# One attention and two expert layers on one core: q and k copied out in key order, the log rows loaded already repeated, and every task of the attention with its own rank and engine

## The chip, the core and the metric

The kernel runs on one core of a Trainium2 chip. The metric is the device time of one execution in microseconds (us); for the kernel before there are three timed runs, and one more execution was profiled.

The engines are named as in the profile: PE is TensorE (its matrix products; its weight loads are listed as PEld), DVE is VectorE, ACT is ScalarE, POOL is GpSimd, and SP is SyncE, which issues nearly all transfers. Each engine runs its own list of instructions in a fixed order; if the instruction at the head of a list waits, everything behind it waits too.

## The reference

Attention over 2 batches of 8 heads, 576 positions and 64 columns, with a bias made by a small network from the distance of two positions; the result goes as 1152 rows of 512 through two layers of two matrix products each (512 to 2048 and back). Cut to what matters:

```python
def _attn_ref(q, k, v, w1, b1, w2):
    scores = scale * np.matmul(q, k.transpose(0, 1, 3, 2))
    psi_rel = np.log1p(np.abs(rel))
    psi_i = np.log1p(np.maximum(pos[:, None], 1.0))
    x = (psi_rel / psi_i)[..., None]
    h = np.maximum(x @ w1 + b1, 0.0)
    bias = h @ w2
    scores = scores + bias.transpose(2, 0, 1)[None, :, :, :]
    attn = softmax(scores)
    return np.matmul(attn, v)

def _moe_ref(x, w_in, w_out, s, b):
    r = np.maximum(x @ w_in, 0.0)
    return (s * (r * r) + b) @ w_out

def _moe2_ref(x, w_in, w_out):
    h = x @ w_in
    sp = log1p(exp(min(h, 20)))
    return (h * np.tanh(sp)) @ w_out
```

Everything is 32-bit floating point at the interface. Each weight of the two layers arrives in 64 bits and is turned into two 32-bit parts on the core.

## The kernel before

**The bias.** The bias depends on the positions only. It is made in 36 groups of 16 query positions (G). For a group, four "rows" are made (`bias_row`, lines 261 to 271: a ReLU of the log row `lx` plus a column of `bl`, 128 partitions by 304 to 576 columns), then PE multiplies them by `w2b` (`bias_products`, L281, in one or two pieces), then the product is copied out of PSUM with a factor (`bias_out`, the tile `bo`; its instruction stands at the helper's lines L172 or L174/L176), then the part on the other side of the diagonal is a mirrored copy inside `bo` (`bias_mirror`, also L172), and then `bo` is stored to memory (`bias_store`, L307, tensor `nbias_d`). It is read back in another layout as `nb` (`load_bias`, L323) when a unit of the attention needs it.

**The start.** Two log rows of 576 numbers are loaded into one partition each (L225). PE spreads them over 128 partitions by a product with ones (L242), and the small network's weights likewise (`c`, L236); DVE and ACT copy these out and scale them (L243 to L251, L172, L176).

**The pairs.** Two heads of one batch make a pair; there are eight. q and k of a pair are loaded (`raw`, L354; for the first two pairs straight into `nat`, L350), regrouped by one copy on ACT (`pack`, `nat` from `raw`), turned by PE (`turn`, L389, tile `t`), and copied out to `qk` (`put`, lines 394 to 402). Column t·64+p of the turned tile belongs to key p·9+t, so the copy reorders: before, it reads PSUM straight through and writes to SBUF with a step of nine elements.

**The units.** A unit is a pair and a tile of queries: tiles 0 to 3 have 128 queries, tile 4 has 64, of which both heads are taken together. There are 40 units. For each: scores on PE (L428, tile `s`), bias and minimum on DVE (L438, tile `mn`), exponential and its sum on ACT (L448, tile `e`), the sum's reciprocal on POOL and DVE (L455, L459, tile `rs`), division on POOL (L465), turning on PE (L480, tile `pp`, and L481/L483, tile `pr`), the copies out (`keep`, tile `pt`; `keep_rest`, tile `prt`; on DVE or ACT), the product with V on PE (L508, tile `po`), and the split of the result into a high and a low part (`xh` on ACT, L528; `xl` on DVE, L168). V is loaded by four transfers a pair (`natv`, L374 and L376: two of 128 KB and two of 16 KB for the last 64 keys), with two clearings on POOL (L371, L372).

**The layers.** Two layers of 48 blocks: products into `h` (L830), an activation on ACT and DVE, products into `y` (L907). Four blocks' first products stand among the last units of the attention.

**What sets the order.** All of it is a list of tasks with an engine, an estimated duration, a rank, the tasks it comes after and the buffers it takes. A planner (`Plan.run`, lines 590 to 623) walks through them: of all tasks that could start, the one that can start first is next, and among equals the one with the lowest rank. The instructions are written out in that order, and each engine keeps it. Before, a task's rank is ten times its unit's number plus a constant of its kind (`RANK`), and the engine of a copy comes from a short repeated pattern:

```python
    ROWS = ('vvav',)
    KEEPS = 'avv'
    OUTS = 'aaa'
    PUTS = 'avv'
```

Here `a` stands for ACT, `v` for DVE, `p` for POOL. So every `bias_out` is on ACT, and of 36 mirrored copies all but the last.

## Time and profile before

| | before |
|---|---|
| median of three runs | 607.04 us (603.47 to 608.15) |
| the profiled execution, its own time | 607.61 us |
| its span in the profile | 605.8 us |
| PE busy | 582.0 us (96%), 4732 matrix instructions |
| DVE busy | 477.0 us (79%) |
| ACT busy | 379.8 us (63%) |
| POOL busy | 86.6 us (14%) |
| moved by DMA | 65.41 MB, mean 108 GB/s |

The span runs from the first to the last instruction of the profile; the execution's own time is 1.8 us more. PE's busy time covers matrix products that overlap in its pipeline, so a stretch in which PE is busy all the time may still hold fewer products than it could. The chain of waits that ends last runs through PE's products of the two layers.

### The profile page before, as it was taken

How to read it: one execution, taken by the hardware profiler on the slowest of the kernel's cores; microseconds unless marked ns; L12 is line 12 of the kernel's file. 1: busy time of each engine (PE TensorE's matmuls, PEld its weight loads, DVE VectorE, ACT ScalarE, POOL GpSimd, SP SyncE). 2: the span in 40 equal slices, each digit the busy share in tenths (PEclk: the TensorE clock that was granted, in tenths of full speed). 3: DMA queues.
4: the chain of work that ended last, by engine and by line, in shares of the span. 5: the costliest groups of instructions: out<-in, count | busy, mean ns of one | idle time of the engine just before them, and what ended most of it. 6: DMA issues, size and time to landing. Idle time of an engine off the chain costs nothing. (4 is left out here: it accounts for less than half of the span.)

```text
span 605.8 us, 12603 instructions
## 1 busy us (share of the span) xinstructions
PE 582.0 (96%) x4732; PEld 511.0 (84%) x4732; DVE 477.0 (79%) x1052; ACT 379.8 (63%) x802; POOL 86.6 (14%) x209
## 2 busy tenths in 40 slices
...
GB/s 98 229 232 256 153 199 153 194 224 169 133 93 102 243 252 252 270 61 1 0 2 1 83 232 240 244 36 1 2 1 0 53 1 1 2 52 1 1 1 52
DMA packets 50064, 65.41 MB, mean 108 GB/s; under 512 B 17490, under 2 KB 34002, under 8 KB 50004
## 3 DMA queue, kind: packets, MB, share of 16 engines
...
q14 instruction: 23, 0.19, 0.1%
q10 hardware_dynamic: 192, 0.09, 0.1%
...
## 5 line engine op out<-in xcount | busy, mean ns | idle before, releaser
L465 POOL TENSOR_SCALAR e<-e,rs 128x576 f32<-128x576 f32 (+2 forms) x104 | 69.0, 680 | 33.9 <-DVE rs L459 29.8
L830 PE MATMUL h<-xh,whi 128*128 128x384 f32 x192 | 64.8, 338 | 0.0
L830 PE MATMUL h<-yh,wli 128*128 128x384 f32 x192 | 64.7, 337 | 0.0
L830 PE MATMUL h<-yl,whi 128*128 128x384 f32 x192 | 64.6, 337 | 0.0
L830 PE MATMUL h<-yh,whi 128*128 128x384 f32 x192 | 64.6, 336 | 0.0
L830 PE MATMUL h<-xh,wli 128*128 128x384 f32 x192 | 64.4, 336 | 0.0
L830 PE MATMUL h<-xl,whi 128*128 128x384 f32 x192 | 64.4, 336 | 0.0
L438 DVE CUSTOM_DVE_ANT_0 s<-s,nb 128x576 f32<-128x576 f32 x72 | 51.9, 753 | 9.2 <-PE s L428 8.1
L428 PE MATMUL s<-qk 64*128 64x144 f32 (+1 forms) x640 | 51.3, 301 | 7.1 <-ACT qk L172 5.4
L428 PEld LDWEIGHTS s<-qk 64*128 64x128 f32 (+1 forms) x640 | 42.0, 179 | 18.8 <-issue 6.8
L448 ACT ACTIVATE e<-s,mn 128x576 f32<-128x576 f32 x72 | 55.5, 772 | 3.1 <-DVE mn L438 2.5
L859 ACT ACTIVATE r<-n,two 128x384 f32<-128x384 f32 x48 | 29.5, 616 | 43.7 <-DVE n L855 43.7
L843 DVE SCALAR_TENSOR_TENSOR u<-h,u 128x384 f32<-128x384 f32 x48 | 26.6, 555 | 36.9 <-ACT u L840 36.8
L271 DVE TENSOR_SCALAR r<-lx,bl 128x528 f32<-128x528 f32 (+17 forms) x108 | 47.4, 486 | 5.5 <-PE bias L281 5.4
L840 ACT ACTIVATE u<-h 128x384 f32<-128x384 f32 x48 | 23.3, 485 | 43.3 <-PE h L830 43.3
L281 PE MATMUL bias<-r,w2b 128*32 128x264 f32 (+17 forms) x352 | 41.0, 526 | 4.8 <-DVE r L271 2.0
L907 PE MATMUL y<-gl,who 128*128 128x384 f32 (+1 forms) x192 | 44.6, 338 | 0.0
L851 ACT ACTIVATE u<-u 128x384 f32<-128x384 f32 x48 | 25.1, 523 | 31.0 <-DVE u L848 30.9
L907 PE MATMUL y<-gh,wlo 128*128 128x384 f32 (+1 forms) x192 | 44.3, 337 | 0.0
L907 PE MATMUL y<-gh,who 128*128 128x384 f32 (+1 forms) x192 | 44.3, 337 | 0.0
L907 PE MATMUL y<-who,gh 128*128 128x512 f32 x144 | 43.3, 395 | 0.9 <-ACT y L919 0.9
L907 PE MATMUL y<-wlo,gh 128*128 128x512 f32 x144 | 43.3, 395 | 0.0
...
## 6 DMA issues: line engine op xcount, KB each, us to landing
...
nb<-nbias_d SPq DMA_DIRECT2D x32, 288.0 KB, 3.3
...
raw<-in_q_dram SPq DMA_DIRECT2D x6, 288.0 KB, 4.0
raw<-in_k_dram SPq DMA_DIRECT2D x6, 288.0 KB, 4.8
```

Source lines behind the costliest of these rows:

```text
L271: engine.tensor_scalar(r, src, bl[:, g : g + 1], 0.0, op0=ALU.add, op1=ALU.max)
L281: nc.tensor.matmul(ps[32 * a : 32 * a + 32], w2b.rearrange("p h i -> p (h i)"), rows[G, a][:, c0:c1], start=True, stop=True)
L428: nc.tensor.matmul(self.ps[rows, x if self.both else 2 * j + x, o : o + PIECE], st.qk[d, 0, self.q0 : self.q0 + self.w], st.qk[d, 1, c0 : ...
L438: nc.vector.tensor_tensor_reduce(out=self.s[n][:m], in0=self.ps[:m, 2 * n : 2 * n + 2, :HALF], in1=nb[:m].rearrange("p (n j) -> p n j", n= ...
L448: nc.scalar.activation(out=self.e[:m, (S + REST) * n :][:, :S], in_=self.s[n][:m].rearrange("p n j -> p (n j)"), func=AF.Exp, bias=self.mn ...
L465: nc.gpsimd.tensor_scalar(self.e[:m, y : y + w], self.e[:m, x : x + w], self.rs[:m, n : n + 1], 0.0, op0=ALU.mult, op1=ALU.add)
L830: nc.tensor.matmul(self.ph, w[:, c * P : (c + 1) * P], x[:, c, :], start=(c == 0 and n == 0), stop=(c == KD - 1 and n == 2),)
L840: nc.scalar.activation(out=self.u, in_=self.ph, func=AF.Relu)
L843: nc.vector.scalar_tensor_tensor(self.u, self.ph, 0.0, self.u, op0=ALU.max, op1=ALU.mult)
L851: nc.scalar.activation(out=self.z, in_=self.z, func=AF.Exp)
L859: nc.scalar.activation(out=self.r, in_=self.n, func=AF.Ln, bias=two)
L907: nc.tensor.matmul(o, a, c, start=(f == 0 and i == 0), stop=(f == NF - 1 and i == 2))
```

## The change

- The log rows and the small weights are loaded by transfers that read the same source again for each partition (`spread`), so that the start needs no product on PE; scaling is on DVE, and `w2b` is filled by four small copies on POOL.
- `put` reads PSUM with a step of 64 elements and writes `qk` straight through, where it read straight through and wrote with a step of nine.
- The last 64 keys of V of both heads of a pair come in one transfer of 128 partitions (`lastv`), and POOL copies them to their places and clears the rest (`spread_v`); before, two transfers went straight there.
- The last part of a unit's turning is a task of its own (`turn_rest`).
- Each task of the attention has its own addition to its rank (`SHIFT`, one character a task, six units a step) and each copy its own engine (`WHO`). The order of the units, several leads and ranks, and the planner's durations are other numbers.

What is computed is the same. In the tables of the diff only a line or two stand.

```diff
-    ROWS = ('vvav',)
-    ROWS0 = ('vvva',)
-    KEEPS = 'avv'
-    RESTS = 'va'
-    OUTS = 'aaa'
-    PUTS = 'avv'
-    PACKS = 'a'
+    WHO = {
...
+        'bias_out': 'vvaaaaavvvvaaaaaaaaaavavaaaaaavaavavaavvvavv',
...
+        'put': 'avaaavavavavavvvvaaa',
...
+    SHIFT = {
...
+        'bias_out': '+/++@-+,7(<+?`7>Vb/J1]8Su5`:,EUu118UC2SL/g9^',
...
+    SSTEP = 6
-    ORDER = ((4, 2), (4, 0), (4, 3), (0, 3), (0, 0), (4, 1), (3, 1), (0, 2), (1, 1), (0, 1), (1, 2), (3, 2), (3, 3), (2, 2), (2, 3), (2, 1), (2, 0), (1, 3), (1, 0), (3, 0))
+    ORDER = ((4, 2), (4, 0), (4, 1), (0, 2), (0, 1), (4, 3), (3, 1), (3, 3), (1, 1), (0, 0), (1, 2), (0, 3), (1, 0), (2, 1), (2, 0), (1, 3), (2, 2), (2, 3), (3, 2), (3, 0))
...
-    NLEAD = 7
+    NLEAD = 5
...
-    FREE = {"PE": 5.6, "ACT": 5.9, "DVE": 5.4, "POOL": 1.5, "SP": 2.1, "none": 0.0}
+    FREE = {"PE": 4.0, "ACT": 5.0, "DVE": 5.4, "POOL": 4.5, "SP": 2.4, "none": 0.0}
...
-    R0 = 9
-    MIRR0 = 35
...
-    WSTEP = 0.89
+    WSTEP = 1.19
...
-    WEARLY = ('i0', 'o0', 'i2', 'o1', 'i1', 'o3', 'o2', 'i3')
+    WEARLY = ('i2', 'o0', 'i1', 'i0', 'o3', 'o1', 'i3', 'o2')
...
-    FRANK = 8
+    FRANK = 2
...
-    GRANK = -443
+    GRANK = -487
...
-    VRANK = 507
+    VRANK = 413
...
-    c1 = bp.tile([HID, 2 + H], F32, name="c1")
     c3 = bp.tile([P, 2 + H], F32, name="c3")
     w1c, b1c = c3[:, 0:1], c3[:, 1:2]
-    lx1 = [rp.tile([1, S], F32, tag="r", name=f"lx1_{n}") for n in range(2)]
-    for n in (1, 0):
-        nc.sync.dma_start(out=lx1[n], in_=ins["c_lx"][n : n + 1])
+
+    def spread(engine, out, src, ap):
+        engine.dma_start(out=out, in_=bass.AP(tensor=src.tensor, offset=src.offset, ap=ap))
+
     with nc.allow_non_contiguous_dma(reason="a few short columns"):
-        nc.sync.dma_start(out=c1[:, 0:1], in_=ins["w1"].rearrange("o (c e) -> (o c) e", e=1))
-        nc.sync.dma_start(out=c1[:, 1:2], in_=ins["b1"].rearrange("(c e) -> c e", e=1))
-        nc.scalar.dma_start(out=c1[:, 2:], in_=ins["w2"])
-    nc.scalar.dma_start(out=liall, in_=ins["c_li"])
+        spread(nc.scalar, w1c, ins["w1"], [[0, RI], [1, HID], [1, 1]])
+        spread(nc.sync, lx[1], ins["c_lx"][1:2], [[0, P], [1, S]])
+        spread(nc.scalar, b1c, ins["b1"], [[0, RI], [1, HID], [1, 1]])
+        nc.scalar.dma_start(out=liall, in_=ins["c_li"])
+        spread(nc.sync, c3[:, 2:], ins["w2"], [[0, RI], [H, HID], [1, H]])
+        spread(nc.sync, lx[0], ins["c_lx"][0:1], [[0, P], [1, S]])
     nc.scalar.preload_act_table_set("natural_log_exp_and_others")
     w2b = bp.tile([P, H, RI], F32, name="w2b")
-    nc.gpsimd.memset(w2b, 0.0)
-    c4 = ps1("c4")[:, : 2 + H]
-    for i in range(RI):
-        nc.tensor.matmul(c4[HID * i : HID * i + HID], ident[:HID, :HID], c1, start=True, stop=True)
-    lx2 = ps4("lx2")
-    ones = rp.tile([1, P], F32, tag="bo", name="ones", bufs=BUFS["bo"])
-    nc.gpsimd.memset(ones, 1.0)
-    for n in (1, 0):
-        for x in range(2):
-            nc.tensor.matmul(lx2[:, 2 * n + x, :HALF], ones, lx1[n][:, x * HALF : x * HALF + HALF], start=True, stop=True)
-    nc.vector.tensor_copy(c3, c4)
-    for i in range(RI):
-        rows = slice(i * HID, (i + 1) * HID)
-        copy("a", w2b[rows, :, i], c4[rows, 2:])
     bl = bp.tile([P, NG], F32, name="bl")
-    nc.vector.tensor_scalar_mul(bl, li, b1c)
-    for n, who in ((1, "v"), (0, "a")):
-        copy(who, lx[n].rearrange("p (x s) -> p x s", x=2), lx2[:, 2 * n : 2 * n + 2, :HALF], w1c)
+    with tc.manual_schedule(engines={mybir.EngineType.DVE, mybir.EngineType.Pool}):
+        nc.gpsimd.memset(w2b, 0.0)
+        nc.vector.tensor_scalar_mul(lx[1], lx[1], w1c)
+        nc.vector.tensor_scalar_mul(bl, li, b1c)
+        nc.vector.tensor_scalar_mul(lx[0], lx[0], w1c)
+        for i in range(RI):
+            rows = slice(i * HID, (i + 1) * HID)
+            nc.gpsimd.tensor_scalar(w2b[rows, :, i], c3[rows, 2:], 1.0, 0.0, op0=ALU.mult, op1=ALU.add)
...
-    def bias_row(G, a):
+    def bias_row(G, a, who):
...
-        who = row_engine(G, a)
...
-    def bias_out(G, c0, c1):
+    def bias_out(G, c0, c1, who):
...
-        copy(OUTS[G % len(OUTS)], bo[G][:, b0 + c0 : b0 + c1], bo[G, c0], ninv[:, G : G + 1])
...
+        copy(who, bo[G][:, b0 + c0 : b0 + c1], bo[G, c0], ninv[:, G : G + 1])
-    def bias_mirror(G):
+    def bias_mirror(G, who):
...
-        if gorder.index(G) < MIRR0:
+        if who == "a":
...
-            nc.gpsimd.memset(a[REST:, FULL, 0, :], 0.0)
-            nc.gpsimd.memset(a[: P - REST, FULL, 1, :], 0.0)
             for j in range(2):
                 nc.sync.dma_start(out=a[:, :FULL, j, :], in_=s2[j, : FULL * P, :].rearrange("(t p) d -> p t d", p=P))
+            self.last_v = natp.tile([P, D], F32, tag="lastv", name=f"lastv_{self.name}")
+            nc.sync.dma_start(out=self.last_v, in_=s2[:, FULL * P :, :])
+            self.v = a
+
+        def spread_v(self):
             for j in range(2):
-                nc.sync.dma_start(out=a[REST * j : REST * j + REST, FULL, j, :], in_=s2[j, FULL * P :, :])
-            self.v = a
+                for x in range(2):
+                    rows = slice(ROW * x, ROW * x + ROW)
+                    if x == j:
+                        nc.gpsimd.tensor_scalar(self.v[rows, FULL, j, :], self.last_v[rows], 1.0, 0.0, op0=ALU.mult, op1=ALU.add)
+                    else:
+                        nc.gpsimd.memset(self.v[rows, FULL, j, :], 0.0)
...
-            to = self.qk.rearrange("d x (p t) -> d x t p", t=DEAL)
+            to = self.qk.rearrange("d x (p t) -> d x p t", t=DEAL)
             if x == 2:
-                copy(who, to[:, :, DEAL - 1], self.last.rearrange("d (x p) -> d x p", x=2))
+                copy(who, to[:, :, :, DEAL - 1], self.last.rearrange("d (x p) -> d x p", x=2))
             elif self.wide:
                 ps = self.ps.rearrange("d n c -> d (n c)")[:, 2 * BANK * x :][:, :S]
-                copy(who, to[:, x], ps.rearrange("d (t p) -> d t p", p=SD))
+                copy(who, to[:, x], ps.rearrange("d (t p) -> d p t", p=SD))
             else:
-                copy(who, to[:, x, : DEAL - 1], self.ps[:, x].rearrange("d (t p) -> d t p", p=SD))
+                copy(who, to[:, x, :, : DEAL - 1], self.ps[:, x].rearrange("d (t p) -> d p t", p=SD))
...
-            self.pr = ps1(f"pr_{self.name}")
...
+        def turn_rest(self):
+            self.pr = ps1(f"pr_{self.name}")
...
         def add(self, engine, us, rank, f, *args, after=(), takes=(), mb=0.0):
+            what = f.__qualname__.split("<locals>.")[-1]
+            n = self.count[what] = self.count.get(what, -1) + 1
+            if what in SHIFT and n < len(SHIFT[what]):
+                rank += SSTEP * (ord(SHIFT[what][n]) - ord("P"))
             t = Task(engine, us, rank, f, args, after, takes, self.LAGS[engine], mb)
+            t.what, t.ways = what, None
             self.tasks.append(t)
+            return t
+
+        def add_any(self, ways, rank, f, *args, **more):
+
+            what = f.__qualname__.split(".")[-1]
+            n = self.count.get(f.__qualname__.split("<locals>.")[-1], -1) + 1
+            who = WHO[what][n % len(WHO[what])]
+            t = self.add(*ways[who], rank, f, *args, who, **more)
+            t.ways = ways
             return t
...
-            add(*(("ACT", 0.0008 * w + 0.1) if row_engine(G, a) == "a" else ("DVE", 0.0007 * w + 0.05)), at - 15 + a,
-                bias_row, G, a, after=[], takes=[hs[a]])
+            add_any({"a": ("ACT", 0.00083 * w + 0.19), "v": ("DVE", 0.0007 * w + 0.05)}, at - 15 + a, bias_row, G, a, takes=[hs[a]])
...
-        m = add(*(("ACT", 0.0008 * (BW - w) + 0.15) if x < MIRR0 else ("POOL", 0.0008 * (BW - w) + 0.25)), at + GRANK + 2, bias_mirror, G, after=outs)
-        stores[G] = add("SP", 0.38, at - 50, bias_store, G, after=[m], mb=0.3)
+        m = add_any({"a": ("ACT", 0.0008 * (BW - w) + 0.1), "p": ("POOL", 0.0012 * (BW - w) + 0.15)}, at + GRANK + 2, bias_mirror, G, after=outs)
...
-                valued[u.hp, u.b] = add("SP", 1.85, 10 * i + VRANK, stacks[u.hp, u.b].load_v, after=[load], mb=0.4)
-                valued[u.hp, u.b].past = [s]
+                hl = Hold("lastv")
+                lv = add("SP", 1.9, 10 * i + VRANK, stacks[u.hp, u.b].load_v, after=[load], takes=[hl], mb=0.4)
+                lv.past = [s]
+                valued[u.hp, u.b] = add("POOL", 0.5, 10 * i, stacks[u.hp, u.b].spread_v, after=[lv])
+                hl.users.append(valued[u.hp, u.b])
...
-        t = add("PE", 0.68 if u.n == 2 else 0.54, at + RANK["turn"], u.turn, after=ds, takes=[hp, hr])
+        t = add("PE", 0.49 if u.n == 2 else 0.27, at + RANK["turn"], u.turn, after=ds, takes=[hp])
+        t1 = add("PE", 0.13 if u.n == 2 else 0.24, at + RANK["turn"] + 1, u.turn_rest, after=ds, takes=[hr])
```

What this does to the order of the instructions, at three places. Line numbers differ between the two kernels (L281 is L308 after, L389 is L423, L428 is L462, L480/L481 are L513/L517, L508 is L544, L268 is L295, and the helper's L172 is L207). Of names like `s_0_2_2962` the first two numbers are the pair's heads and the query tile, the last is a running number; both batches have the same name.

The first instructions of PE, before:

```order
L1081 UNCONDITIONAL_BRANCH
L242 MATMUL lx_134<-lx_1_119,ones 128x288 x2
L242 MATMUL lx_134<-lx_0_118,ones 128x288 x2
L236 MATMUL c_129<-c_116,ident 32x10 x4
L281 MATMUL bias_0_179<-r_169,w2b 32x264
L281 MATMUL bias_0_179<-r_171,w2b 32x264
```

and now:

```order
L1129 UNCONDITIONAL_BRANCH
L308 MATMUL bias_0_166<-r_151,w2b 32x264
L308 MATMUL bias_0_166<-r_156,w2b 32x264
L308 MATMUL bias_0_166<-r_158,w2b 32x264
L308 MATMUL bias_0_166<-r_162,w2b 32x264
```

The eight products that spread the rows and the weights are gone; the first bias group is PE's first work.

The first instructions of ACT after its table load, before (`bo` from `bias` is a copy out, `bo` from `bo` a mirrored copy):

```order
L172 ACTIVATE w2b<-c_129 32x8 x4
L172 ACTIVATE lx_113<-lx_134,c_117 128x576
L268 ACTIVATE r_175<-lx_114,bl 128x528
L172 ACTIVATE bo_193<-bias_0_179,li 128x264
L268 ACTIVATE r_195<-lx_114,bl 128x544
L172 ACTIVATE bo_193<-bias_264_186,li 128x264
L172 ACTIVATE qk_2_198<-t_2_197 128x9x64
L172 ACTIVATE bo_193<-bo_193 128x63
L172 ACTIVATE bo_236<-bias_0_220,li 128x272
```

and now:

```order
L295 ACTIVATE r_151<-lx_114,bl 128x528
L295 ACTIVATE r_158<-lx_114,bl 128x528
L295 ACTIVATE r_164<-lx_114,bl 128x544
L295 ACTIVATE r_182<-lx_114,bl 128x544
L295 ACTIVATE r_185<-lx_114,bl 128x560
L207 ACTIVATE bo_180<-bo_180 128x63
L207 ACTIVATE qk_2_188<-t_2_187 128x576
L207 ACTIVATE bo_225<-bias_0_210,li 128x272
L207 ACTIVATE bo_225<-bias_272_219,li 128x272
L207 ACTIVATE bo_225<-bo_225 128x47
```

ACT makes two rows of each of the first two groups instead of one, and the first group's two copies out are on DVE. Up to ACT's ninth exponential its list holds 31 rows instead of 23, 22 copies out instead of 30, 13 mirrored copies instead of 21, nine copies of `qk` of 512 or 576 columns and two of 128 instead of eight and none, four `pt` copies of 512 columns instead of two, and three `prt` copies instead of two. DVE's list up to its ninth minimum holds 63 rows instead of 68, eight copies out instead of none, seven large and two small `qk` copies instead of eight and four, and one `pt` copy instead of three.

PE late in the attention, before, some ten units ahead of the end:

```order
L428 MATMUL s_0_2_2962<-qk_0_755 128x144 x8
L480 MATMUL pp_1_2_2975<-ident,e_1_2_2838 128x64 x16
L481 MATMUL pr_1_2_2976<-ident,e_1_2_2838 128x128
L508 MATMUL po_3_2_3004<-pt_3_2_2959,natv_3_1014 64x128 x8
L508 MATMUL po_3_2_3004<-prt_3_2_2953,natv_3_1014 64x128 x2
L428 MATMUL s_3_1_3026<-qk_3_841 128x144 x8
L480 MATMUL pp_1_2_3039<-ident,e_1_2_2895 128x64 x16
L481 MATMUL pr_1_2_3040<-ident,e_1_2_2895 128x128
L508 MATMUL po_1_2_3070<-pt_1_2_3015,natv_1_1315 64x128 x8
L508 MATMUL po_1_2_3070<-prt_1_2_3024,natv_1_1315 64x128 x2
```

and now, from the same scores:

```order
L462 MATMUL s_0_2_2724<-qk_0_737 128x144 x8
L544 MATMUL po_0_1_2740<-pt_0_1_2664,natv_0_833 64x128 x8
L544 MATMUL po_0_1_2740<-prt_0_1_2681,natv_0_833 64x128 x2
L544 MATMUL po_1_2_2762<-pt_1_2_2738,natv_1_894 64x128 x8
L544 MATMUL po_1_2_2762<-prt_1_2_2718,natv_1_894 64x128 x2
L513 MATMUL pp_1_2_2782<-ident,e_1_2_2649 128x64 x16
L462 MATMUL s_3_1_2805<-qk_3_539 128x144 x8
L517 MATMUL pr_1_2_2821<-ident,e_1_2_2649 128x128
L513 MATMUL pp_0_2_2829<-ident,e_0_2_2722 128x64 x16
L462 MATMUL s_3_1_2855<-qk_3_956 128x144 x8
L517 MATMUL pr_0_2_2873<-ident,e_0_2_2722 128x128
L544 MATMUL po_1_2_2875<-pt_1_2_2814,natv_1_1019 64x128 x8
```

The fixed round of scores, turn and values is gone: the order differs from unit to unit, and other products stand between the two parts of a turn. The products of the two layers keep their order but for a few places.

## Rows read from the trace of the kernel before

**Rows 1.** Busy time by stretch: stretch, us, each engine (instructions), PE clock, DMA share, GB/s
```profile
0.00:8.55 8.55, 4.41 (x17) 2.72 (x18) 2.08 (x7) 2.63 (x7) 1.13 (x10) 1.00 0.57 126
8.55:78.14 69.59, 56.18 (x668) 29.07 (x669) 48.77 (x118) 55.43 (x115) 9.85 (x29) 0.93 0.69 198
78.14:205.55 127.41, 125.79 (x1933) 103.72 (x1934) 116.00 (x309) 103.05 (x263) 72.13 (x144) 1.00 0.53 166
205.55:605.80 400.25, 395.62 (x2116) 375.47 (x2115) 310.13 (x620) 218.68 (x421) 3.53 (x26) 1.00 0.23 73
```

**Rows 2.** PE in order of time: the ninth group of scores, then one dense round
```profile
78.14 1.25 PE L428 MATMUL s<-qk 64*128 64x144 f32 x16
...
89.50 1.20 PE L428 MATMUL s<-qk 64*64 64x144 f32 x16
90.62 0.71 PE L480 MATMUL pp<-ident,e 64*128 64x64 f32 x16
...
92.77 0.80 PE L281 MATMUL bias<-r,w2b 128*32 128x352 f32 x8
93.50 1.25 PE L428 MATMUL s<-qk 64*128 64x144 f32 x16
```

**Rows 3.** All engines in order of time, the start: start us, us, instruction, idle before
```profile
0.73 0.63 SPq L225 DMA_DIRECT2D lx<-in_c_lx_dram  x2
...
6.85 0.29 DVE L248 TENSOR_SCALAR bl<-li,c 128x144 f32<-128x144 f32 x1
...
7.06 0.81 DVE L176 TENSOR_SCALAR lx<-lx,c 128x576 f32<-128x576 f32 x1
7.91 0.74 ACT L172 ACTIVATE lx<-lx,c 128x576 f32<-128x576 f32 x1 [0.26 <-DVE lx L176]
7.91 3.97 DVE L271 TENSOR_SCALAR r<-lx,bl 128x528 f32<-128x528 f32 x9
...
8.55 2.74 PE L281 MATMUL bias<-r,w2b 128*32 128x264 f32 x16 [1.97 <-DVE r L271]
```

**Rows 4.** DMA issues by line: KB each, median us from issue to landing
```profile
nb<-nbias_d SPq DMA_DIRECT2D x32, 288.0 KB, 3.3
...
raw<-in_k_dram SPq DMA_DIRECT2D x6, 288.0 KB, 4.8
```

**Rows 5.** Instructions by helper line, 0 to 80 us, and the rows `r`: ns min/median/max
```profile
L172 ACT ACTIVATE bo<-bias,li x30: 461/502/690, 10.4 to 77.5; 128x264 f32<-128x264 f32 x4, 128x272 f32<-128x272 f32 x4, 128x280 f32<-128x280 f32 x4, 128x288 f32<-128x288 f32 x4
...
L172 ACT ACTIVATE bo<-bo x22: 206/282/361, 13.5 to 78.8; 128x63 f32<-128x63 f32 x2, 128x47 f32<-128x47 f32 x2, 128x31 f32<-128x31 f32 x2, 128x15 f32<-128x15 f32 x2
L172 ACT ACTIVATE qk<-t x8: 1068/1170/1217, 12.5 to 73.2; 128x576 f32<-128x576 f32 x4, 128x512 f32<-128x512 f32 x4
...
L172 ACT ACTIVATE pt<-pp x2: 576/584/591, 34.9 to 62.3; 128x512 f32<-128x512 f32 x2
...
L174 DVE COPY qk<-t x8: 1069/1140/1210, 13.7 to 72.1; 128x576 f32<-128x576 f32 x4, 128x512 f32<-128x512 f32 x4
...
L271 DVE TENSOR_SCALAR r<-lx,bl x108: 368/453/1069, 7.9 to 124.8; 128x528 f32<-128x528 f32 x6, 128x544 f32<-128x544 f32 x6, 128x560 f32<-128x560 f32 x6, 128x576 f32<-128x576 f32 x6
L268 ACT ACTIVATE r<-lx,bl x36: 538/651/767, 8.5 to 123.8; 128x528 f32<-128x528 f32 x2, 128x544 f32<-128x544 f32 x2, 128x560 f32<-128x560 f32 x2, 128x576 f32<-128x576 f32 x2
```

**Rows 6.** In order of time: two copies of one pair, the scores that wait
```profile
35.02 1.20 PE L428 MATMUL s<-qk 64*64 64x144 f32 x16 [0.79 <-ACT qk L172]
...
50.98 1.87 PE L428 MATMUL s<-qk 64*64 64x144 f32 x16 [2.04 <-ACT qk L172]
...
58.69 2.18 PE L428 MATMUL s<-qk 64*64 64x144 f32 x16 [2.52 <-ACT qk L172]
```

**Rows 7.** Two five-us stretches (as rows 1), and one bias product at two times
```profile
50.00:55.00 5.00, 4.03 (x32) 1.99 (x32) 2.65 (x9) 2.81 (x4) 0.00 (x0) 0.66 1.05 319
60.00:65.00 5.00, 5.00 (x34) 1.80 (x30) 2.04 (x5) 2.71 (x6) 0.00 (x0) 0.50 0.65 165
...
33.21 1.01 PE L281 MATMUL bias<-r,w2b 128*32 128x480 f32 x8 [0.31 <-ACT bo L172]
...
62.04 1.83 PE L281 MATMUL bias<-r,w2b 128*32 128x480 f32 x8
```

84 lines of the change are left out of this document (59 added, 25 removed).

## The prediction

> **What bounds the kernel now.** I read the busy times by stretch first, cut at two places: the ninth group of scores, which starts at 78.14 us, and 205.55 us, where PE begins the products into `y`. The reader is to see three different machines [rows 1]. After 205.55 PE is busy 395.62 of 400.25 us, and the change leaves these products alone. From 78.14 to 205.55 it is busy 125.79 of 127.41 us; 1.6 us could be had there. Before 78.14 it is busy 4.41 of 8.55 us (with the products that only spread the constants) and 56.18 of 69.59 us. So what a better order can give lies in the first 78 us.
>
> Busy PE is not dense PE, so next I read one dense round in order of time [rows 2]: scores at 89.50, turn at 90.62, a bias product of 352 columns at 92.77, next scores at 93.50. Scores take 1.12 us of PE, turn and values together 2.15, the bias 0.73, or 2.07 ns a column. Ahead of the ninth scores stand 22 bias groups (10,896 columns, as the copies out of the order say: 22.6 us), eight scores (9.0), the turns of eight pairs (about 7, taken at 0.9 like a unit's) and the turn and values of five or six small units (about 8, at two thirds of 2.15). That is 47 us of dense work in 69.6 us: some 23 us are lost there, 13.4 of them as plain idleness, the rest in products that start one by one as their rows come, or at a lower clock.
>
> What are they lost to? ACT is busy 55.43 of the 69.59 us, DVE 48.77 [rows 1]; ACT is the fullest engine but idle for 14.2 us. PE's longest waits are scores that wait for the second copy of `qk`, 0.79, 2.04 and 2.52 us [rows 6]. And the clock: from 60 to 65 us the granted clock is 0.50, the lower level of 1.2 GHz, from 50 to 55 us 0.66 on average, after PE had stood still before the scores at 50.98 and 58.69 [rows 6, 7]. A bias product of 480 columns took 1.01 us at 33.21 and 1.83 us at 62.04 [rows 7].
>
> **The change part by part.**
>
> *The start.* Before, PE's first bias product begins at 8.55, behind a spread by PE and a copy of 0.81 us [rows 3]. Now two transfers of 295 KB each do the spreading. The nearest row is `nb`, as large and in as many rows, 3.3 us from issue to landing [rows 4]; issued at about 0.73, the first lands at 4.0. DVE then needs 0.81 for the row and 0.29 for `bl` [rows 3], so ACT can start its first row at 5.1; the second log row and its 0.81 us bring DVE's own first row to 5.9, and with 0.44 us for it (nine in 3.97 us [rows 3]) PE starts at 6.35. Gain 2.2 us. Bounds: if the transfers land like the slowest loads of that size, 4.8 us [rows 4], the gain is 0.7; if DVE needs for a row from SBUF no more than for an `r` (0.44), it is 2.9.
>
> *ACT's list up to its ninth exponential.* By the counts under the order and the durations of [rows 5]: eight rows more (+5.2 at 0.651), eight copies out fewer (-4.0 at 0.502), eight mirrored copies fewer (-2.3 at 0.282), two `pt` copies more (+1.2 at 0.584), the four `w2b` copies and the `lx` copy gone (-1.4: 0.74 for `lx` [rows 3], the rest a quarter of it each). The `qk` copies: eight at 1.17 are 9.4 us now. After the change they write straight through but read PSUM with a step of 64 elements. No row shows such a read. One bound is the `lx` copy of the same 576 columns from PSUM, straight on both sides: 0.74 us on ACT and 0.81 on DVE [rows 3]; the other is no change, 1.17. I take the first, since the row nearest in shape and size shows what the copy costs without any step, and the write is the side from which the step goes. Then nine copies at 0.74 and two small ones at 0.28 (a mirrored copy's) make 7.2: -2.2. Sum for ACT: 5.2 - 4.0 - 2.3 + 1.2 - 1.4 - 2.2 = -3.5, and with one more `prt` copy (at a mirrored copy's 0.28) -3.2. DVE: five rows fewer (-2.3), eight copies out more (+3.6, at 0.81 for 576 columns and in proportion), one `lx` more (+0.8), `qk` -4.3 (eight at 1.14 become seven at 0.81, two small ones go), two `pt` copies fewer (-1.4): -3.6. So both lists get shorter, and neither takes the other's place. As ACT is the fullest, its 3.2 us count in full; if the time is set by other waits they count nothing.
>
> In a rule of the Trainium skill, page "SBUF — State Buffer", section "Door 1: The DMA port swizzle", SBUF serves accesses that stay in one line of 16 bytes at full rate and pays for each new line, and PSUM has lines of 8 bytes. The first half agrees with the 1.17 us for a write with a step of 36 bytes. The second half speaks against the change: a step of 256 bytes in PSUM would be as bad as what it replaces. By it these terms are nothing; that is the third rival.
>
> *The scores that wait.* The two copies of a pair run one after the other, so a pair's chain shortens by twice about 0.4 us. Of the waits of 0.79, 2.04 and 2.52 us [rows 6] it takes 2.4 at most. I count 2.0; nothing, if the copies cost what they did.
>
> *The clock.* Against the upper level the slow stretch cost 0.8 us in the 480 columns [rows 7], which come twice, 0.7 and 1.0 in the scores of 1.87 and 2.18 us (1.20 at 35.02 [rows 6]): with the 448 columns between them, priced alike at half a microsecond to a piece of eight, some 4 us. With shorter waits before it the clock should hold longer. I count 3.0 of 4; nothing at worst.
>
> *V, the turns and POOL.* One transfer instead of two for the last keys of a pair saves SP an issue, eight in all, and adds a short POOL task ahead of a pair's first values; POOL is busy only 9.85 of 69.59 us [rows 1]. Nothing either way. The mirrored copies that go to POOL lie between product and store; a DVE-side delay from them is in the last rival. Values wait for V behind this task; queued behind it on POOL are divisions, which are wanted one unit later.
>
> *The dense stage.* ACT has 103.05 of 127.41 us there, DVE 116.00, POOL 72.13 [rows 1]. DVE sheds eight rows and six large `pt` copies to ACT and takes eight copies out; ACT's share rises to about 84%, DVE's falls to about the same. PE stays the bound with the same products: nothing.
>
> Sum: 2.2 + 3.2 + 2.0 + 3.0 = 10.4 us. The profiled execution took 607.61 us, its span 605.8; the median of the three runs is 607.04, so the execution is an ordinary one. 607.6 - 10.4 = 597.2; I predict 597. The ninth scores, or the same amount of work, then stand at about 68 us.
>
> **The rivals.**
>
> *More than that.* The 14.2 us in which ACT stands idle [rows 1] could shrink to half if every wait of the start were arranged away, and the clock could hold throughout: 7 us more, 590. For it: 23 us are lost there by the dense count. Against: by 78.14 us about 14.9 MB are moved (8.55 us at 126 GB/s, 69.59 at 198 [rows 1]), and the two spread rows add 0.6. To be there at 61 us takes 15.5 MB at 254 GB/s from the first moment; the fullest five us show 319 at a share above 1 [rows 7].
>
> *Transfers hold it.* The same sum on the other side: with 198 GB/s, as now, 15.5 MB take 78 us, and stores and loads stand in one SP list in fixed order. Then only the start and half of ACT's part remain: 2.2 + 1.6, 603.8. For it: DMA's share of 0.69 over the whole stretch. Against: it is an average with idle phases.
>
> *The copies stay slow.* If a stepped PSUM read costs as much, 2.2 of ACT's term and 2.0 of the waits go, 601.4; and part of the clock's with them.
>
> *Slower.* Before, PE's late order is a fixed round, in which each product was ready when its turn came. Now it differs from unit to unit; a wait of PE for a turn, a copy or a division stops all behind it. After the ninth scores 31 more units follow. From 0.34 us of wait in each the 10.4 us are used up; at 0.8 us each it is 607.6 - 10.4 + 24.8 = 622, at 0.53 us just 1% slower (613.6); I put it at 614. What would cause it is POOL, on the way to each turn: it has 20 mirrored copies now, by the order, instead of one. An `r` on DVE took 1069 ns at the longest against a median of 453 [rows 5], so the two do slow each other somewhere. The Trainium skill, page "GPSIMD Engine Reference", section "Key points", says that POOL shares its SBUF interfaces with DVE and contends with DVE instructions in a 2-port mode or with two SBUF inputs. Against it: POOL has 55 us free in this stage, DVE and ACT 11 and 24 [rows 1].
>
> **How the numbers follow.** A measurement of this kernel can tell about 1%, 6 us, from no change. Forecast (591 to 601.5) 0.56; more (under 591) 0.14; transfers 0.13; slow copies 0.08; slower 0.09. Faster by over 1%: the forecast, the first rival and half of the slow copies, 0.74. Same: 0.13 + 0.04 = 0.17. Slower: 0.09. The range of 587 to 606 leaves out the best part of the slower case and the lower end of the first rival; the forecast's own range is 591 to 601.5.
>
> **What would show it.** In the profile after: PE's first bias product near 6.4 us; `qk` copies near 0.75 us; the ninth scores near 68 us; a granted clock of 1.00 between 50 and 65 us for most of the time; and from there to the first `y` still about 127 us. Wrong would be: copies above 1.1 us; the ninth scores after 74 us; waits of PE for `pp`, `pt` or `e` of more than 10 us in the dense stage; or idle PE after the first `y`.

## The result, and the profile after

The changed kernel takes 599.95 us (median of 4 runs, 599.38 to 602.0) against 607.6 (4 runs), a ratio of 0.9893 with a 95% interval of 0.9859 to 0.9926. The prediction was 597 us with a range of 587 to 606. The profiled execution of the changed kernel took 602.0 us with a span of 600.2, so it is the longest of its four; its single times below are good to about 2 us.

Busy time by stretch, changed kernel, cut at its first bias product (8.71), its ninth scores (70.31) and its first product into `y` (198.25); columns as in [rows 1]:

```profile
0.00:8.71 8.71, 0.00 (x0) 0.03 (x1) 1.79 (x7) 2.16 (x3) 1.69 (x11) 1.00 0.56 150
8.71:70.31 61.60, 54.16 (x682) 28.80 (x684) 45.50 (x115) 52.50 (x111) 17.04 (x51) 0.94 0.80 229
70.31:198.25 127.94, 125.57 (x1928) 102.66 (x1925) 110.09 (x297) 108.98 (x265) 73.60 (x159) 1.00 0.53 165
198.25:600.20 401.95, 395.56 (x2113) 374.76 (x2112) 309.24 (x620) 217.26 (x419) 4.82 (x26) 1.00 0.22 73
```

Against [rows 1] the reader is to see one stretch that differs: the ninth scores come 7.8 us earlier. The stretch behind them is 127.94 us against 127.41, and the expert layers are 401.95 against 400.25, though their instructions are the same; over the kernels below this last stretch scatters between 400.2 and 402.6 for no reason that I found. ACT's busy time up to the ninth scores fell from 58.06 to 54.66 us, DVE's from 50.85 to 47.29.

The start, all engines in order of time, answers to [rows 3]:

```profile
0.73 1.16 ACTq L259 DMA_DIRECT2D c<-in_w_dram  x1
...
1.91 0.55 ACTq L259 DMA_DIRECT2D c<-in_b_dram  x1
...
2.49 0.49 ACTq L265 DMA_DIRECT2D li<-in_c_li_dram  x1
...
3.99 0.52 DVE L273 TENSOR_SCALAR lx<-lx,c 128x576 f32<-128x576 f32 x1 [3.13 <-DMA lx<-in_c_lx_dram]
...
7.50 0.30 DVE L274 TENSOR_SCALAR bl<-li,c 128x144 f32<-128x144 f32 x1 [2.99 <-DMA li<-in_c_li_dram]
...
8.71 0.71 PE L308 MATMUL bias<-r,w2b 128*32 128x264 f32 x2 [8.71 <-ACT r L295]
```

The spread log row is there at 3.99, as predicted, and PE starts no earlier than before (8.55): `bl` waits until 7.50 for `li`, whose load is the third in ACT's queue.

The copies of `qk`, by line and shape: busy us, mean ns of one, and idle time ahead of them; they answer to the `qk` lines of [rows 5]:

```profile
L209 DVE COPY qk<-t 128x576 f32<-128x576 f32 x5 | 3.7, 756 | 4.9 <-PE t L423 3.8 <-ACT qk L207 1.2
L207 ACT ACTIVATE qk<-t 128x512 f32<-128x512 f32 x6 | 3.3, 595 | 0.0
L207 ACT ACTIVATE qk<-t 128x576 f32<-128x576 f32 x3 | 2.0, 652 | 0.5 <-PE t L423 0.4 <-DVE qk L209 0.2
L209 DVE COPY qk<-t 128x512 f32<-128x512 f32 x2 | 1.4, 688 | 0.2 <-ACT qk L207 0.2
L207 ACT ACTIVATE qk<-l 128x128 f32<-128x128 f32 x2 | 0.8, 394 | 0.0
```

They took 1170 and 1140 ns (medians) and take 595 to 756.

Two five-us stretches that answer to [rows 7], and one in which the clock is low now:

```profile
35.00:40.00 5.00, 4.85 (x46) 2.37 (x46) 2.46 (x6) 3.14 (x9) 1.57 (x6) 0.62 0.91 238
50.00:55.00 5.00, 3.84 (x55) 2.18 (x49) 4.34 (x11) 3.52 (x6) 0.81 (x2) 1.00 1.04 299
60.00:65.00 5.00, 4.78 (x57) 2.45 (x53) 3.44 (x11) 4.99 (x14) 3.25 (x12) 1.00 0.96 279
```

And where the waits in [rows 6] stood, PE in order of time:

```profile
32.77 2.18 PE L462 MATMUL s<-qk 64*64 64x144 f32 x16 [1.54 <-ACT qk L207]
34.88 1.88 PE L308 MATMUL bias<-r,w2b 128*32 128x496 f32 x8
...
51.67 1.20 PE L462 MATMUL s<-qk 64*64 64x144 f32 x16 [1.16 <-DVE qk L209]
...
70.31 1.20 PE L462 MATMUL s<-qk 64*128 64x144 f32 x16
```

The stretches at 50 and 60 us run at a granted clock of 1.00 (0.66 and 0.50 before). But the low clock is not gone: it sits behind the third scores, where PE stood idle from 31.2 to 32.8; scores take 2.18 us there.

How long PE's scores waited for `qk`, from 8 us to the ninth scores (us in total, times, longest), before and then after:

```profile
PE s L428 <- ACT qk L172: 5.4, 3, 2.5
PE s L428 <- DVE qk L174: 0.8, 1, 0.8
```

```profile
PE s L462 <- ACT qk L207: 1.5, 1, 1.5
PE s L462 <- DVE qk L209: 1.2, 1, 1.2
```

These waits fell from 6.2 to 2.7 us. From the first bias product to the ninth scores the stretch is 8.0 us shorter, and the rows of busy time part this: PE is idle for 7.4 us there instead of 13.4, and busy for 54.2 instead of 56.2.

The view that I had not read before the prediction is the one of SP's waits, of before up to its ninth scores, and then of the changed kernel up to its own (us in total, times, longest):

```profile
SPq L307 <- ACT bo L172: 23.7, 10, 6.4
SPq L354 <- ACT bo L172: 1.9, 2, 1.4
SPq L354 <- DMA raw<-in_k_dram: 1.8, 1, 1.8
```

```profile
SPq L334 <- ACT bo L207: 10.1, 6, 2.8
SPq L334 <- POOL bo L330: 3.2, 3, 1.2
SPq L381 <- ACT bo L207: 2.5, 1, 2.5
```

SP issues its list in a fixed order, and a store of a bias (L307, L334) that waits for its `bo` holds back each load behind it. Over all rows of the two views SP stood still for 31.2 us before and 25.8 after. But these windows end at different times. The last `raw` load of k ahead of the ninth scores is issued at 54.98 before and at 49.42 after, and up to there SP stood still for 19.7 and 18.4 us: 1.3 of the 5.6 us. The rest is what stands ahead of that load: 61 transfers before, which take 35.1 us to issue, and 51 after, which take 30.3. Of the 5.6 us, 3.9 lie between the k loads of the last two pairs (6.4 us before, 2.5 after), in SP's own order of time, first before and then after:

```profile
48.59 0.60 SPq L354 DMA_DIRECT2D raw<-in_k_dram  x1
...
50.41 0.56 SPq L323 DMA_DIRECT2D nb<-nbias_d  x1
51.01 1.61 SPq L374 DMA_DIRECT2D natv<-in_v_dram  x2
53.07 1.14 SPq L376 DMA_DIRECT2D natv<-in_v_dram  x2
...
54.98 1.72 SPq L354 DMA_DIRECT2D raw<-in_k_dram  x1
```

```profile
46.92 0.60 SPq L381 DMA_DIRECT2D raw<-in_k_dram  x1
47.57 1.07 SPq L334 DMA_DIRECT2D nbias_d<-bo  x2
48.76 0.61 SPq L381 DMA_DIRECT2D raw<-in_q_dram  x1
49.42 1.06 SPq L381 DMA_DIRECT2D raw<-in_k_dram  x1
```

Before, a load of `nb` and the four transfers of a pair's V stand between these two loads; now they come later.

Of the 7.8 us that the ninth scores gained, 5.6 are there when this load is issued, and 2.3 come in the chain from it (23.16 us to the ninth scores before, 20.89 after). That this load is what the ninth scores wait for is argued and not shown: kernel 3 below issues it 4.4 us later than the changed kernel and has its ninth scores 3.4 us earlier, with 37 fewer products of PE ahead of them.

### The profile page after: what moved, and what is told of

Same layout as the page of the kernel before. It is cut to its first block, busy times and chain, and to the rows that moved or that the text cites. A ratio compares the mean times of both kernels' runs of the same rounds, so it can differ in the third digit from the quotient of the medians.

```text
span 600.2 us, 12549 instructions
## 1 busy us (share of the span) xinstructions
PE 575.3 (96%) x4716; PEld 506.3 (84%) x4716; DVE 466.6 (78%) x1036; ACT 380.9 (63%) x794; POOL 97.2 (16%) x247
## 4 chain that ended last, share of the span: by engine, by line
PE 74%; DVE 11%; ACT 6%; DMA 4%; issue 3%; POOL 1%; ACTq 0%; DVEq 0%; POOLq 0%
PE y L955 28%; PE h L878 27%; PE po L544 6%; PE s L462 6%; PE pp L513 3%; PE bias L308 3%; DMA rawi<-in_moe_w_in_dram 2%; PE pr L517 1%; DVE r L298 1%; ACT r L295 1%; DVE wlo L203 1%; DVE wfi L190 1%; DVE wfo L190 1%; DMA nbias_d<-bo 1%; ACT bo L207 1%
## 5 line engine op out<-in xcount | busy, mean ns | idle before, releaser
L499 POOL TENSOR_SCALAR e<-e,rs 128x576 f32<-128x576 f32 (+2 forms) x104 | 65.3, 643 | 23.0 <-DVE rs L493 16.8
L462 PE MATMUL s<-qk 64*128 64x144 f32 (+1 forms) x640 | 50.1, 297 | 5.6 <-ACT qk L207 1.5
L462 PEld LDWEIGHTS s<-qk 64*128 64x128 f32 (+1 forms) x640 | 41.9, 179 | 13.0 <-DVE qk L209 2.0
L308 PE MATMUL bias<-r,w2b 128*32 128x264 f32 (+17 forms) x352 | 38.6, 509 | 10.2 <-ACT r L295 8.7
L899 ACT ACTIVATE u<-u 128x384 f32<-128x384 f32 x48 | 24.9, 521 | 32.8 <-DVE u L896 32.7
L298 DVE TENSOR_SCALAR r<-lx,bl 128x464 f32<-128x464 f32 (+17 forms) x95 | 42.5, 491 | 1.8 <-PE bias L308 1.7
## 6 DMA issues: line engine op xcount, KB each, us to landing
natv<-in_v_dram SPq DMA_DIRECT2D x16, 128.0 KB, 3.6
```

The lines of the kernel that those rows point to most:

```text
L298: engine.tensor_scalar(r, src, bl[:, g : g + 1], 0.0, op0=ALU.add, op1=ALU.max)
L308: nc.tensor.matmul(ps[32 * a : 32 * a + 32], w2b.rearrange("p h i -> p (h i)"), rows[G, a][:, c0:c1], start=True, stop=True)
L462: nc.tensor.matmul(self.ps[rows, x if self.both else 2 * j + x, o : o + PIECE], st.qk[d, 0, self.q0 : self.q0 + self.w], st.qk[d, 1, c0 : ...
L499: nc.gpsimd.tensor_scalar(self.e[:m, y : y + w], self.e[:m, x : x + w], self.rs[:m, n : n + 1], 0.0, op0=ALU.mult, op1=ALU.add)
L899: nc.scalar.activation(out=self.z, in_=self.z, func=AF.Exp)
```

## The experiments

My theory after the result was this: the gain comes from the copies of `qk` and from the order, which puts the loads earlier in SP's list; the start gives nothing. Its rivals: the order alone, or the copies alone. Twelve kernels were run, each timed beside the kernel before (606.56 us, median of 26 runs, for the first four; 606.15, 18 runs, for the next; 607.29, 11 runs, for the last). In the table, "k load" is when the last `raw` load of k ahead of the ninth scores is issued, "S9" the ninth scores, "dense" the stretch from there to the first product into `y`, each in us in the profiled execution.

| kernel | median | ratio to before, 95% | first bias | k load | S9 | dense |
|---|---|---|---|---|---|---|
| before | 607.6 | | 8.55 | 54.98 | 78.14 | 127.4 |
| changed | 599.95 | 0.9893, 0.9859 to 0.9926 | 8.71 | 49.42 | 70.31 | 127.9 |
| 1 changed, old copies | 606.32 | 1.0003, 0.9982 to 1.0024 | 8.68 | 49.92 | 73.88 | 127.9 |
| 2 before, new copies | 602.75 | 0.9928, 0.9901 to 0.9955 | 8.57 | 53.60 | 72.79 | 127.4 |
| 3 changed, no tables | 610.03 | 1.0059, 1.0038 to 1.0080 | 8.94 | 53.79 | 66.89 | 138.6 |
| 4 `li` first on ACT | 600.82 | 0.9913, 0.9879 to 0.9946 | 9.10 | 48.47 | 68.61 | 128.0 |
| 5 `li` on SP | 599.83 | 0.9902, 0.9866 to 0.9937 | 6.65 | 48.68 | 68.99 | 127.9 |
| 6 old start | 600.1 | 0.9913, 0.9883 to 0.9943 | 9.51 | 48.84 | 69.75 | 127.9 |
| 7 no ranks | 604.24 | 0.9977, 0.9952 to 1.0001 | 8.81 | 48.88 | 67.55 | 133.8 |
| 8 no step in PSUM | 600.88 | 0.9920, 0.9893 to 0.9948 | 8.75 | 48.47 | 69.30 | 128.0 |
| 9 mirrors on POOL | 601.05 | 0.9898, 0.9873 to 0.9923 | 8.68 | 49.37 | 69.89 | 128.2 |
| 10 and packing on POOL | 601.07 | 0.9901, 0.9876 to 0.9925 | 8.83 | 49.07 | 69.37 | 128.1 |
| 11 k loaded twice | 620.62 | 1.0222, 1.0195 to 1.0249 | 8.70 | 67.23 | 89.33 | 127.9 |
| 12 V as before | 600.66 | 0.9893, 0.9868 to 0.9918 | 8.80 | 48.95 | 70.08 | 127.4 |

**1 and 2, the copies.** The layout of the copies is undone in the changed kernel, or done alone in the kernel before:

```diff
-            to = self.qk.rearrange("d x (p t) -> d x p t", t=DEAL)
+            to = self.qk.rearrange("d x (p t) -> d x t p", t=DEAL)
...
-                copy(who, to[:, x], ps.rearrange("d (t p) -> d p t", p=SD))
+                copy(who, to[:, x], ps.rearrange("d (t p) -> d t p", p=SD))
```

> The changed kernel, but the copies of q and k write with a step of nine elements again, as before; the order of all instructions stays the changed one. Theory one (the gain of some 7.6 us comes from two parts of the first 70 us: shorter q and k copies, which shorten the chain from a pair's turn to its scores, and shorter lists on ACT with a better order): the copies take 1.1 to 1.2 us again instead of 0.61 and 0.76, the ninth scores start 3 to 4 us later (70.3 to about 74), the time is 603.5 (602 to 605.5) against 600 for the changed kernel. Theory two (the order alone): 600, ninth scores within 1 us of 70.3. Theory three (the copies alone): 607, as before.

> The kernel before, with only the copies of q and k in the new form (reads PSUM with a step of 64, writes straight through). Theory one: ninth scores 3 us earlier than 78.1, time 604 (602 to 606). Theory two: 607. Theory three: 600.

Without the new copies nothing of the gain is left (606.32, as the theory of the copies alone had it); with them alone, 0.7% of the 1.1% is there (602.75, in the range of theory one, where the copies alone were to give 600). By line and shape, first the changed kernel with old copies, then the kernel before with new ones:

```profile
L207 ACT ACTIVATE qk<-t 128x512 f32<-128x512 f32 x6 | 6.3, 1126 | 0.1
L209 DVE COPY qk<-t 128x576 f32<-128x576 f32 x5 | 5.8, 1198 | 5.9 <-PE t L423 3.4 <-ACT qk L207 2.5
```

```profile
L174 DVE COPY qk<-t 128x576 f32<-128x576 f32 x4 | 3.0, 755 | 4.1 <-PE t L389 2.8 <-ACT qk L172 1.3
L172 ACT ACTIVATE qk<-t 128x512 f32<-128x512 f32 x4 | 2.4, 593 | 0.4 <-DVE qk L174 0.4
```

Same bytes, in 53% of the time on ACT and 63% on DVE. PE's waits of scores for `qk`, up to the ninth scores, again first kernel 1 and then kernel 2:

```profile
PE s L462 <- DVE qk L209: 3.0, 2, 2.4
PE s L462 <- ACT qk L207: 2.5, 1, 2.5
```

```profile
PE s L428 <- ACT qk L172: 2.7, 2, 1.5
```

With the old copies they are 6.2 us in the old order and 5.5 in the new one, with the new copies 2.7 in both: this part of the gain belongs to the copies, whatever the order.

The column "k load" belongs to the order: with the new order it is 5.1 (kernel 1) and 5.6 us ("changed") earlier whatever the copies cost, and with new copies alone only 1.4. From that load to the ninth scores it takes 23.2 us before, 24.0 in kernel 1, 20.9 changed and 19.2 in kernel 2: the copies take 3.1 to 4.0 off. So in the trace all but the copies brings 4.3 us to the ninth scores (78.14 to 73.88), and in the timed runs it brings nothing. The trace compares two single executions: 1.7 us of the 4.3 are longer later stretches (dense 0.5, layers 1.2), the profiled execution of before (607.61) is 1.05 above the median of those 26 runs, and that of kernel 1 (605.03, the lowest of its 12) is 1.3 below its own. What is left is the 0.2 us between the two medians. So an earlier k load by itself is shown to be worth nothing here. On top of the new copies the order may be worth something (0.9928 for kernel 2, 0.9893 for the changed one), but these intervals overlap, and kernels 4 to 6, 8 to 10 and 12, with the same two tables, lie between 0.9893 and 0.9920: up to 0.35%, which these runs do not tell from nothing.

**3 and 7, the tables.** Kernel 7 takes the added ranks away and keeps the engines; kernel 3 also deals the tasks by the patterns of before:

```diff
-            if what in SHIFT and n < len(SHIFT[what]):
+            if False:
...
-            who = WHO[what][n % len(WHO[what])]
+            who = old_engine(what, n, args)
```

> The changed kernel without its two tables: each task has the rank of its kind, and copies take their engines from the old repeated patterns; start, copies of q and k, V's load, split turn, unit order and constants are the changed ones. Theory one: the copies' part is left, the order's is gone, 604 (601 to 607), ninth scores near 75. Theory two: 607 or more. Theory three: 600.

> The changed kernel with the table of ranks off and the table of engines kept. With both tables off the ninth scores were at 66.9 us, and the stretch from there to the first y took 138.6 us instead of 127.9 (610.0 us in all). Theory one (the ranks keep the dense stage dense, the engines only even out the loads): the stretch again takes 135 us or more, 607 to 612 us. Rival (the engines did it): the stretch takes 128 to 130 us, 600 to 602 us.

Kernel 3 missed what I had expected, 604 us and ninth scores near 75. The ninth scores are the earliest of all there, and the dense stage loses it again; stretch by stretch, kernel 3 and then kernel 7:

```profile
66.89:205.50 138.61, 130.66 (x1954) 103.02 (x1955) 120.74 (x319) 108.17 (x273) 71.93 (x148) 1.00 0.51 160
```

```profile
67.55:201.30 133.75, 129.09 (x1952) 103.83 (x1953) 110.41 (x304) 110.78 (x272) 78.08 (x159) 1.00 0.54 165
```

Part of the early ninth scores is order: 645 and 652 products of PE stand ahead of them, 682 in the changed kernel. But from there PE is idle for 8.0 and 4.7 us (2.4 in the changed kernel), and busy for 5.1 and 3.5 us more. DVE's 120.74 us fall to 110.41 with the engines' table. By the ratios to before, the engines' table is worth 0.8% (1.0059 to 0.9977) and the ranks as much again (to 0.9893), some 5 us each. This is their worth within the changed kernel, whose unit order and constants are new too; it is not what the change gained over the order of before, since kernel 3 is slower than that. In kernel 7 theory one held in direction, with less than its 135 us and 607.

**4, 5 and 6, the start.** `li` issued first on ACT, or on SP behind the first log row (shown), or the whole start of before:

```diff
         spread(nc.sync, lx[1], ins["c_lx"][1:2], [[0, P], [1, S]])
+        nc.sync.dma_start(out=liall, in_=ins["c_li"])
         spread(nc.scalar, b1c, ins["b1"], [[0, RI], [1, HID], [1, 1]])
-        nc.scalar.dma_start(out=liall, in_=ins["c_li"])
```

> The changed kernel with the load of li issued as ACT's first transfer instead of its third. In the changed kernel DVE waits 3.0 us for li before bl, and PE's first bias product starts at 8.71 us, no earlier than before. Theory one: bl is made by about 5 us, the first bias product starts near 6.3, and as all later work of the start follows from it, the ninth scores come 2 us earlier and the time is 598 (597 to 599). Rival (transfers hold the first 70 us: their share there is 0.80, and above 0.9 in many stretches): the lead is used up in waits for loads by the third scores, 600.

> The changed kernel with li's load issued on SP, behind lx[1] and ahead of the rest, so that only w1 and b1 stand in ACT's queue and nothing small is its third transfer. Theory one (the start was lost because the third transfer of ACT's queue lands at 7.5 to 7.9 us beside the large loads): li and b1 land by 5.0 us, bl is made by 5.5, the first bias product starts at 6.5 to 7.0 instead of 8.71, the ninth scores come 1 to 2 us earlier than 70.31, and the time is 598 us, ratio 0.987 to before. Rival (small transfers land late in any queue as soon as the large loads run): li or b1 still lands after 7 us, the first product is at 8.5 or later, 600 us. Second rival (the start is early but hidden, as the transfers of the first 40 us set the pace): first product before 7.2, ninth scores still at 70 us, 600 us.

> The changed kernel with the start of before: one-row loads, the spreading of w1, b1, w2 and the log rows by PE and the copies out of PSUM on ACT and DVE. Theory one (the new start gives nothing, since its first product is at 8.71 us against 8.55): 600 us within 1.5, ratio 0.988 to before, first bias product at 8.5. Rival (the copies of the old start, some 1.4 us of ACT and 1.6 of DVE, and its PE work do count, as the prediction had it): 602 to 603 us, ninth scores 2 us later than 70.31.

In kernel 4 `li` came early and then `b1`, now third in ACT's queue, was waited for until 7.89: the first product did not move (9.10), and the time was 600.82 us, not 598. Kernel 5 made the start that I had predicted, all engines in order of time:

```profile
5.44 0.30 DVE L274 TENSOR_SCALAR bl<-li,c 128x144 f32<-128x144 f32 x1 [0.36 <-DMA c<-in_b_dram]
...
6.65 2.51 PE L308 MATMUL bias<-r,w2b 128*32 128x264 f32 x16 [6.65 <-ACT r L295]
...
10.37 1.19 PE L423 MATMUL t<-ident,nat 64*128 64x64 f32 x17 [0.83 <-DMA nat<-in_k_dram]
...
27.04 1.20 PE L462 MATMUL s<-qk 64*64 64x144 f32 x16 [0.97 <-DVE mn L472]
```

It is two us earlier at the first product, 0.2 at the second scores (27.26 in the changed kernel): the turn waits for its `nat` load, and the second scores for `mn`, which waits for a bias that is stored and loaded again. The time is that of the changed kernel, and so it is with the start of before, first product at 9.51. The ninth scores are 1.3 us earlier (68.99), but kernel 4, with the latest first product but one, has them at 68.61, so this is no effect of the start. The second rival of kernel 5 held in what came of it, the start is hidden; the reason that it gave, the pace of the transfers, was not tested.

**8, the step in PSUM.** The copies read straight through; the keys of q and k are then in no useful order, so this kernel leaves out the reordering and its results are not those of the reference:

```diff
-                copy(who, to[:, x], ps.rearrange("d (t p) -> d p t", p=SD))
+                copy(who, to[:, x], ps.rearrange("d (p t) -> d p t", t=DEAL))
```

> The changed kernel with its large q and k copies reading PSUM straight through (keys in no useful order, so what is computed differs in the order of keys of q and k); writes as they are. Same bytes, same engines, no step of 64 elements on the PSUM side. Theory one (the stepped read costs nothing): the copies keep 607 ns on ACT and 757 ns on DVE (medians, within 5%), 600 us. Rival (it costs a part, by the rule of lines of 8 bytes): they fall to under 520 and 650 ns, and the time by up to 1 us.

They took 596 and 652 ns on ACT and 687 and 756 on DVE (512 and 576 columns), within 1 ns of the changed kernel's. A read of PSUM with a step of 64 elements (256 bytes) costs these copies nothing.

**9 and 10, ACT's list.** The mirrored copies, and then the packing copies of q and k too, run on POOL, in the same order:

```diff
-        if who == "a":
-            copy("a", dst, src[:, ::-1])
-        else:
-            nc.gpsimd.tensor_scalar(dst, src[:, ::-1], 1.0, 0.0, op0=ALU.mult, op1=ALU.add)
+        nc.gpsimd.tensor_scalar(dst, src[:, ::-1], 1.0, 0.0, op0=ALU.mult, op1=ALU.add)
...
-            if who == "p":
+            if True:
```

> The changed kernel with every mirrored copy on POOL, in the place that the order gives it; 15 of them leave ACT, some 13 of these before the ninth scores at 0.27 us each, 3.5 us. In the changed kernel ACT is busy for 15.98 of the 16.0 us from 54 to 70 us, four of the mirrored copies among them. Theory one (ACT's list is what paces the last part before the ninth scores): these come 1 to 2 us earlier than 70.31, 598.5 us. Rival (transfers or the chain of copies pace it): no change within 1 us, 600 us, or later by what POOL takes longer for a copy.

> As the last, and the six packing copies of q and k (1.16 us each on ACT) on POOL too. Theory one (ACT's list paces it): ACT falls by another 4.6 us in its four packing copies between 45 and 59 us, ninth scores 3 us earlier than 70.31, 597 us. Rival (the chain of a pair from its load to its scores paces it, through packing, turn and copies): POOL takes 1.5 to 2.5 us for a packing copy, so the fourth to ninth scores come later, 601 to 605 us.

The stretch from the first bias product to the ninth scores of kernel 10, and its packing copies:

```profile
8.83:69.40 60.57, 53.05 (x684) 27.95 (x684) 46.66 (x116) 44.80 (x92) 27.49 (x69) 0.97 0.81 232
```

```profile
L387 POOL TENSOR_SCALAR nat<-raw 128x1152 f32<-128x1152 f32 x6 | 7.3, 1218 | 6.9 <-DMA raw<-in_k_dram 6.8
```

ACT does 7.7 us less than in the changed kernel, and the ninth scores come 0.9 us earlier; the time is the same within 1.2 us. In kernel 9, where 16 mirrored copies leave ACT (not 15), ACT does 1.9 us less (3.5 expected), and they come 0.4 us earlier. Theory one of both expectations falls: the fullest engine does not set this stretch. The last load of k is issued at 49.37 and 49.07, as in the changed kernel (49.42): the stores that hold SP now wait for the mirrored copies on POOL. The rival's price was wrong too: POOL packs in 1.22 us, not 1.5 to 2.5, against 1.16 on ACT, so the chain of a pair got no longer and its rival was not put to the test.

**11, k loaded twice.**

```diff
-            nc.sync.dma_start(
+            for _ in range(1 + x):
+                nc.sync.dma_start(
...
```

> The changed kernel with the raw load of k issued twice for the six later pairs: 1.77 MB more, 7.7 us at the 229 GB/s that the stretch from 8.71 to 70.31 us shows, nothing more for any engine but six issues. Theory one (transfers are not what holds the first 70 us; ACT and the chain are): ninth scores at most 2.5 us later, 600 to 602.5 us. Rival (transfers hold it, as DMA's share of 0.9 to 1.0 between 30 and 60 us suggests): 5 to 8 us later, 605 to 608 us.

It cost 20 us, more than either theory allowed, for a reason that I had not thought of; SP's waits up to 90 us:

```profile
SPq L382 <- DMA raw<-in_k_dram: 23.4, 6, 4.3
```

The second load goes to the place of the first and waits in SP's list until that has landed, six times 3.9 us. So this says nothing on how full the DMA engines are. It says that a list held six times comes out late: the ninth scores are 19.0 us later (89.33). It does not say how much of a wait of SP counts, since SP's other waits up to the ninth scores fell from 25.8 to 11.9 us, each of the six pairs also has its k some 4 us later, and the granted clock up to there was 0.89 instead of 0.95.

**12, V as before.** Two transfers and two clearings for a pair's last keys in place of one transfer and a POOL task:

```diff
-            self.last_v = natp.tile([P, D], F32, tag="lastv", name=f"lastv_{self.name}")
-            nc.sync.dma_start(out=self.last_v, in_=s2[:, FULL * P :, :])
+            nc.gpsimd.memset(a[REST:, FULL, 0, :], 0.0)
+            nc.gpsimd.memset(a[: P - REST, FULL, 1, :], 0.0)
+            for j in range(2):
+                nc.sync.dma_start(out=a[REST * j : REST * j + REST, FULL, j, :], in_=s2[j, FULL * P :, :])
...
```

> The changed kernel with V's last keys loaded as before: two transfers of the last 64 keys straight into place and two clearings on POOL for a pair, no task on POOL behind the transfer. Theory one (V's part is worth nothing, as predicted): 600 us within 1.5. Rival (the one transfer spares SP time or queue): 602 us or more.

The one transfer is worth nothing, as predicted. No kernel was faster than the changed one beyond the scatter of 1 to 2 us; kernels 4 to 6, 8 to 10 and 12 all end at 600 to 601.

## Why the prediction was right, and where it was not

The forecast held: faster, 600 for 597, all of it ahead of the ninth scores (70.31, 68 predicted), a dense stage of 127.9 us. That the sum came near is luck in part: of its 10.4 us, the 5.4 of the start and of ACT's list brought nothing by themselves, the clock brought less than was counted, and the waits for `qk` brought more. By its steps:

*The start, 2.2 us: wrong, 0.* I had priced the log rows, whose spread came as predicted, and let `li` and `b1` land as before. `li` took 2.1 us from issue to landing before and 4.9 now. Kernel 5 made the predicted start, 6.65 for 6.35, and it brought nothing: nor had I asked who waits for the first product. The second scores wait for a bias that goes out and in.

*ACT's list, 3.2 us: right in size, wrong in what it does.* ACT's busy time fell by 3.4 us and DVE's by 3.6 (3.6 predicted), though two misses cancel in the first: the eight rows more cost some 0.7 us more than counted, the copies of `qk` some 0.7 less. But "as ACT is the fullest, its 3.2 us count in full" is the step that failed: kernels 9 and 10 took 1.9 and 7.7 us from ACT for 0.4 and 0.9. What gained in its place is the term that I had counted third, the scores that wait for `qk`: 3.5 us less (6.2 to 2.7), where I counted 2.0, and by the copies, as kernels 1 and 2 show. PE's idle time ahead of the ninth scores fell by 6.0 us in all; which change took the other 2.5 is not shown. SP's fixed list, which stood under a rival, gave an earlier k load, and kernel 1 shows no time for that.

*The copies: right, and more than right.* 0.74 and 0.81 us were predicted, 0.65 and 0.76 came for 576 columns; the two small ones cost 0.39, not 0.28. The stretch from the last k load to the ninth scores got 3.1 to 4.0 us shorter by them. The rival of the slow copies is excluded by these times, and kernel 8 shows that the step costs nothing. It stood on the Trainium skill, page "SBUF — State Buffer", section "Door 1: The DMA port swizzle", with its lines of 8 bytes in PSUM. The price that this section names for a read that is not contiguous is one of matmuls; I had carried it over to copies, and for copies by ACT and DVE the trace doesn't show it (596 against 595 ns). With the section's line of 16 bytes in SBUF the trace agrees: kernel 1 writes with a step of 36 bytes and takes 1126 ns for 512 columns on ACT where the changed kernel takes 595.

*The clock, 3.0 us: too much.* Both slow spots of [rows 7] are gone, and one has come up at 33 us. Each timed run comes with its mean granted clock: over the 55 runs of the kernel before that were timed beside the twelve kernels it averages 0.9939, over the four of the changed kernel 0.9955. Of the 55, the six at 1.000 average 603.7 us and the eighteen at 0.992 average 607.7, half a us for each 0.001; so by this estimate the clock gave about 0.8 us. In kernels 4 to 6, 8 to 10 and 12, which take the same time, the 43 runs average 0.9975, which would be 1.8. At a clock of 1.000 kernels 4 to 6 average 598.5 to 599.9 (eight runs): 599.3 against 603.7, so 4.5 us of the gain are there without the clock.

*V, turns, POOL and the dense stage, 0: right.* V was tried by kernel 12; the split turn was not tried by itself. The rival of a slower dense stage did not come: of POOL's 20 mirrored copies 11 lie in that stage, and it takes 127.94 us against 127.41. But kernels 3 and 7 show that it was near. Without the table of ranks that stage takes 6 us more, and without both tables 11, more than the whole gain.

*Transfers hold it.* With a DMA share of 0.80 and 229 GB/s the stretch moves 14.1 MB where it moved 13.8, in less time, so the 198 GB/s before were no limit, and this rival as I put it is excluded. Whether a share of 1.04 from 50 to 55 us now delays a load was not settled, since kernel 11 measured something else.
